# A DeltaNet and mixer kernel on one core: the written-out order of all steps is replaced by another

## The chip, the cores and the metric

The kernel runs on one core of a Trainium2 chip. A core has engines that each run their own instruction stream in order: TensorE (PE in the profile; PEld is its weight load, which overlaps the multiplication), VectorE (DVE), ScalarE (ACT), GpSimd (POOL) and SyncE (SP). Streams meet through semaphores. SP, POOL and, at the very start, ACT also issue the DMA transfers between HBM and the core's memory. The metric is the device time of one execution in microseconds. TensorE's clock is granted by a throttle, and the profile shows the granted clock (1.00 is full).

## The reference

The attention part is a delta rule with a state of 48 x 48 for each of 4 x 8 batches and heads, over 768 positions, everything in fp32; the second part mixes tokens through a rank of 32 and then runs an MLP of 384 to 1536 to 384 over channels:

```
k_n = k / (norm(k) + 1e-06)
for t in range(768):                       # q, k, v: (4, 8, 768, 48)
    y[t]  = q[t] @ state
    v_old = k_n[t] @ state
    state = state + beta[t] * outer(k_n[t], v[t] - v_old)
x  = y as (4, 768, 384)                    # heads side by side
u  = x + (x.T @ U @ V).T                   # U: 768 x 32, V: 32 x 768
out = u + relu(u @ w_ch1) @ w_ch2          # 384 x 1536, 1536 x 384
```

## The kernel before

**The work.** A sequence is cut into 12 chunks of 64 positions; six chunks of one batch's 8 heads are a *unit* n, so there are 8 units, two for each batch. For each unit the kernel

- loads k, q, v and z (a second copy of part of k), lower and upper half apart (`load`, DMA at L310; upper halves go through POOL's queue, lower ones through SP's, and the first unit's upper k through ACT's) and, once, beta (`load_beta`, L322, POOL);
- transposes k and q on PE (L218, copies at L390, L392, L395) and multiplies k by k and q by k in each chunk (`products`, L407, with copies and masks at L411 to L426);
- takes norms and beta into a scale (`norms`: square root on ACT at L353, DVE at L356 to L361) and scales v on DVE;
- inverts a unit triangular matrix for each chunk and head (`blocks`): DVE transposes the diagonal blocks (L459), substitutes column by column with one multiplication (L468) and one subtraction (L469) for each, into a tile `xt` that POOL has filled with zeros (`seed`, L454), and transposes back (L473); then PE joins the small inverses to larger ones (`joins`, L525 to L574, with ACT and DVE between). The first two units are cut into blocks of 16 (15 columns), so that the chain of DVE is short;
- runs over its chunks in order (`recur` and `outputs`, PE at L621, L628, L686, L697, L714, with DVE at L679, L704, L720, L722 and ACT at L611, L689 between). The first two units multiply k and v by the inverse ahead of time (`prepare`, L643 for k and L648 for v, ACT copies at L650, L652).

The second part's weights are loaded and converted (`start` at L790, `load_weights` with three DVE operations L809, L815, L818 and an ACT cast L796 for each of 14 slices; U is the first). For each batch and third of its tokens there are token products and a low-rank term (`front`), the first layer (`channels`, L1126 or, cut in quarters, L206), the relu on ACT (L1096), the second layer (`narrow`, L1214 or L206) and DVE's adding up (`gather`, L1160). The last batch's MLP takes another form (`quick`, L904 with DVE at L889). The second part's work of a batch stands beside the recurrence of the next, so that PE has work while the recurrence waits.

**What sets the order.** Every one of these pieces is a generator, a *part*, that stops at each instruction or short group of instructions (a *step*). A text, `ORDER`, lists one token for each step, 2342 in all. A token is the number of a part, with the PSUM bank where there is one to choose, and a `q` where a step is done in quarters. The run takes the text from left to right:

```
for token in ORDER.split():
    ...
    step = waits[int(i)]
    ...
    advance(int(i), int(bank) if bank else first)
```

So each engine's stream, and each DMA queue's, is exactly the subsequence of the text that falls to it: nothing is moved later by a scheduler. Semaphores are added from the data that instructions share; how many separate semaphore instructions an engine gets depends on the order too. A step that stands in an engine's stream and whose input isn't there holds up everything behind it on that engine.

A square root on ACT needs another function table than a copy. The last step of the first unit's upper k load is a square root of a dummy, `warm` (L315), which no other step reads:

```
if halves == (1,) and (n, name) == (0, 'k'):
    yield op('act')
    nc.scalar.sqrt(warm, warm)
```

## Time and profile before

| | |
|---|---|
| runs before | 583.02, 583.38, 586.18 us (median 583.38) |
| profiled execution, span | 581.3 us from first to last instruction; its own time is not listed apart, the median of the runs is 2.1 us more than the span |
| mean granted TensorE clock | 0.988 |
| busy: PE / PEld / DVE / ACT / POOL | 549.3 / 464.3 / 405.2 / 248.1 / 97.8 us |
| matrix instructions on PE | 11349 recorded |
| bytes moved | 33.38 MB in 63851 packets |

In the rows below, times are microseconds from the first instruction, and a line number such as L407 is a line of the kernel before. A row of the table of stretches has the stretch, its length, the busy time and the number of instructions of PE, PEld, DVE, ACT and POOL, the granted clock, the mean share of the DMA engines that are busy, and GB/s. A row of waits has the engine and line that waited, what it waited for, and us in total, number, and the longest. A row in time has the start, the duration, engine and line, operation, output and input with their shapes, and in brackets how long the engine had been idle and what ended that. A row of costly groups has the group and its count, then busy time and mean ns.

### The profile page before, as it was taken

How to read it: one execution, taken by the hardware profiler on the slowest of the kernel's cores; microseconds unless marked ns; L12 is line 12 of the kernel's file. 1: busy time of each engine (PE TensorE's matmuls, PEld its weight loads, DVE VectorE, ACT ScalarE, POOL GpSimd, SP SyncE). 2: the span in 40 equal slices, each digit the busy share in tenths (PEclk: the TensorE clock that was granted, in tenths of full speed). 3: DMA queues.
4: the chain of work that ended last, by engine and by line, in shares of the span. 5: the costliest groups of instructions: out<-in, count | busy, mean ns of one | idle time of the engine just before them, and what ended most of it. 6: DMA issues, size and time to landing. Idle time of an engine off the chain costs nothing.

```text
span 581.3 us, 25150 instructions
## 1 busy us (share of the span) xinstructions
PE 549.3 (94%) x11349; PEld 464.3 (80%) x11349; DVE 405.2 (70%) x1006; ACT 248.1 (43%) x526; POOL 97.8 (17%) x169
## 2 busy tenths in 40 slices
PE   5766999999999999999999999999999999999997
PEld 4665887669889788789879876989879869656997
DVE  6999875699998239899972899998323248157442
ACT  3678886553333553254245323631531331465000
POOL 8212150260001214221014105200000000000000
PEclk9999689999999999999999999999999999999999
DMA  9997292280000243620014204200000000000010
GB/s 146 171 249 194 75 224 54 56 151 6 30 4 16 46 76 62 111 45 3 30 24 95 61 14 85 54 29 2 31 3 2 31 2 1 28 1 0 15 41 28
DMA packets 63851, 33.38 MB, mean 57 GB/s; under 512 B 50816, under 2 KB 61824, under 8 KB 63744
## 3 DMA queue, kind: packets, MB, share of 16 engines
q1 hardware_dynamic: 56800, 23.21, 18.6%
q0 software_dynamic: 5344, 8.27, 6.6%
q8 instruction: 89, 1.46, 1.1%
q10 hardware_dynamic: 1600, 0.30, 0.3%
q14 instruction: 18, 0.15, 0.1%
HBM read 27.03 MB, written 4.72 MB: 55 GB/s over the span
## 4 chain that ended last, share of the span: by engine, by line
PE 80%; DVE 14%; issue 2%; ACT 1%; DMA 1%; SPq 0%; DVEq 0%; ACTq 0%
PE P L1214 25%; PE P L1126 13%; PE P L206 10%; PE P L904 7%; PE P L407 3%; PE P L951 3%; PE P L218 2%; DVE prod L468 2%; DVE xt L469 2%; PE P L628 2%; PE P L621 2%; PE P L686 2%; PE P L923 1%; PE P L1049 1%; PE P L673 1%
## 5 line engine op out<-in xcount | busy, mean ns | idle before, releaser
L1126 PE MATMUL P<-ut,w_sb 128*128 128x256 f32 x384 | 88.4, 385 | 0.1
L1214 PE MATMUL P<-w_sb,hs 128*128 128x192 f32 x456 | 79.9, 330 | 0.5 <-issue 0.5
L1126 PEld LDWEIGHTS P<-ut,w_sb 128*128 128x128 f32 x384 | 71.3, 190 | 11.1 <-issue 1.2
L1214 PEld LDWEIGHTS P<-w_sb,hs 128*128 128x128 f32 x456 | 74.1, 190 | 2.2 <-issue 1.3
L469 DVE TENSOR_TENSOR xt<-xt,prod 128x112 f32<-128x112 f32 (+21 forms) x200 | 64.6, 323 | 6.9
L468 DVE TENSOR_TENSOR prod<-gs,xt 128x112 f32<-128x112 f32 (+21 forms) x200 | 63.5, 318 | 2.5
L1096 ACT ACTIVATE hs<-P 128x512 f32<-128x512 f32 x48 | 28.7, 597 | 66.9 <-PE P L1126 52.4
L206 PE MATMUL P<-ut,w_sb 64*64 64x256 f32 x768 | 55.9, 383 | 0.9 <-ACT hs L1096 0.6
L1160 DVE TENSOR_TENSOR X<-X,P 128x192 f32<-128x192 f32 x85 | 29.2, 347 | 38.1 <-PE P L1214 35.2
L1214 PE MATMUL P<-w_sb,S 128*128 128x192 f32 x240 | 41.6, 329 | 0.0
L1214 PEld LDWEIGHTS P<-w_sb,S 128*128 128x128 f32 x240 | 39.0, 190 | 0.4
L407 PE MATMUL P<-slot 48*64 48x64 f32 x1536 | 34.6, 244 | 4.0 <-issue 2.0
L611 ACT COPY X<-P 64x192 f32<-64x192 f32 x96 | 30.0, 312 | 15.4 <-PE P L628 13.8
L591 POOL MEMSET slot<- 32x384 f32 x32 | 13.7, 433 | 135.7 <-PE P L562 126.0
L587 ACT COPY slot<-zz 32x384 f32<-32x384 f32 x64 | 32.2, 508 | 10.2 <-DVE zz L473 8.9
L407 PEld LDWEIGHTS P<-slot 48*64 48x64 f32 x1536 | 30.9, 156 | 7.0 <-issue 3.0
L206 PEld LDWEIGHTS P<-ut,w_sb 64*64 64x64 f32 x768 | 27.3, 133 | 9.5 <-issue 2.5
L720 DVE TENSOR_TENSOR s<-s,P 128x192 f32<-128x192 f32 x40 | 14.0, 350 | 29.8 <-PE P L714 25.0
L310 POOL DMA_DIRECT2D slot<-in_q_dram x32 | 20.9, 657 | 80.9 <-DVE prod L468 31.1
L689 ACT COPY z<-P 128x192 f32<-128x192 f32 x36 | 11.4, 318 | 53.2 <-PE P L686 45.9
L310 POOL DMA_DIRECT2D slot<-in_k_dram x44 | 29.0, 667 | 22.2 <-PE P L714 17.3
L889 DVE TENSOR_TENSOR slot<-slot,P 128x384 f32<-128x384 f32 x36 | 19.4, 553 | 19.1 <-PE P L904 18.1
(182 smaller groups left out, 1048.1 us busy)
## 6 DMA issues: line engine op xcount, KB each, us to landing
w_sb<-in_moe_w_ch_dram SPq DMA_DIRECT2D x14, 384.0 KB, 4.3
out_dram<-X SPq DMA_DIRECT2D x22, 192.0 KB, 2.0
slot<-in_k_dram SPq DMA_DIRECT2D x48, 72.0 KB, 4.1
slot<-in_k_dram POOLq DMA_DIRECT2D x44, 72.0 KB, 4.3
slot<-in_q_dram SPq DMA_DIRECT2D x32, 72.0 KB, 4.8
slot<-in_q_dram POOLq DMA_DIRECT2D x32, 72.0 KB, 4.9
slot<-in_v_dram SPq DMA_DIRECT2D x32, 72.0 KB, 3.9
slot<-in_v_dram POOLq DMA_DIRECT2D x32, 72.0 KB, 3.0
```

The costliest lines, as they stand in the source:

```text
L206: nc.tensor.matmul(to[half(g)], w[half(r), half(g)], x[half(r)], start=start, stop=stop, skip_group_check=True)
L310: queue.dma_start(out=t[half(1 - g if name == 'z' else g), :, to, 0:D], in_=src[b, 4 * g + s, hf * UC * L:(hf + 1) * UC * L, :].rearrange( ...
L407: nc.tensor.matmul(p_g[half(g ^ par * i), par, c], kq[rows, c, j, 0, half(g)], kq[rows, c, j, i, half(g)], start=True, stop=True)
L468: nc.vector.tensor_tensor(out=prod, in0=gb[:, :, j:j + 1, j + 1:].to_broadcast([128, split, m, w]), in1=xb[:, :, 0:m, j:j + 1].to_broadcas ...
L469: nc.vector.tensor_tensor(out=xb[:, :, 0:m, j + 1:], in0=xb[:, :, 0:m, j + 1:], in1=prod, op=ALU.subtract)
L587: nc.scalar.copy(pg[quarter(i), :, at, :, a:a + BK], cut(zc, h)[quarter(i)].rearrange('p r (c j) t -> p r c j t', j=2))
L611: nc.scalar.copy(x[half(c % 2), c // 2, 4 * D * g:4 * D * (g + 1)].rearrange('p (j r d) -> p r j d', r=2, d=D), states(p_y)[half(g)])
L904: nc.tensor.matmul(banks[x], w1_sb[:, 4 * a[0] + e, a[1]] if isinstance(a, tuple) else w1_mixes[a][:, e], tokens(*t) if isinstance(t, tupl ...
L1096: nc.scalar.activation(hs[:, fs[0]:fs[1] + 1:fs[1] - fs[0]], p_f, ACTF.Relu)
L1126: nc.tensor.matmul(p_f[:, x], w(x, t), ut[:, t], start=t == 0, stop=t == KT - 1)
L1160: nc.vector.tensor_tensor(out=to, in0=to, in1=p, op=ALU.add)
L1214: nc.tensor.matmul(to, of[0], of[1], start=of[2], stop=of[3], skip_group_check=True)
```

## The change

The text `ORDER` is replaced as a whole (95 lines, now 96); nothing else differs. The new text has the same multiset of steps, with the same 25 choices of quarters; only one choice of a bank differs. Because the text is one line longer, every line of code behind it has a number that is higher by one. Part numbers differ between the texts (parts are numbered as they come to life): in the part of the text shown, 1 and 0 are the first unit's k loads (the fifth token of part 1 is the square root of `warm`), 2 is beta's load with its PE and ACT steps, 147 is the load of U, 26 and 43 the upper z loads of the first two units, 36, 37 and 38, 39 the second unit's k and q, 20 the zero fill of `xt`, 146 the conversion of weights, 19 the first unit's `blocks`. The order was found with a model of the steps that also counts PE's semaphore records when it counts off lots of 256 of its instructions.

Instructions on the engines: 5913 multiplications in both texts, line by line the same; separate semaphore instructions go from 112 to 116 on PE, 136 to 129 on ACT, 177 to 173 on DVE, 62 to 56 on SP and 44 to 46 on POOL. ACT's stream has two loads of a function table instead of one: one for copies at its start, and one for square roots ahead of L353 (L354 in the new file).

```
@@ -50,95 +50,96 @@
     ORDER = """
-    1 0 1 0 1 0 1 0 2 1 36 147 37 21 150 22 36 152 153 151 149 14.3 37 21 201 2 148 201 37 36 22 36 22 21 15.1
-    20 38 202.2 148 203 39 146 148 146 204 203 2 37 21 146 205.0 202 22 154 148 202 26 38 202 29.3 39 205 149
-    39 2.1 38 205 206 205 39 2 19 202 207.3 205 2 2 2 12 17.2 202 12 207 208 19 202 12 19 205 207 19 205 209.0
-    207 19 207 19 207 3.1 19 207 3 19 209 30.2 19 18.3 209 210 19 24 23 3 3 211 19 24 38 19 24 23 3 19 24 25
...
-    714 712 718 718 714 719 715 720 715 721 721 716 722 722 723 723
+    26 147 1 1 0 0 14.0 1 1 0 201 0 15.1 202 36 43 146 37 203 201 204.2 204 202 205.3 37 204 36 36 20 29.0
+    205 206 37 2 2 146 146 38 204 205 2 2.1 2 2 149 2 37 150 43 205 22 22 22 19 22 39 39 12 2 12 19 148 148
+    205 19 19 207.0 39 207 19 19 19 207 36 30.1 208 204 38 209.3 21 21 19 19 148 148 146 19 19 209 207 17.1
+    19 209 19 21 21 39 211 18.2 19 24 209 213 210 19 146 150 209 19 146 155 19 204 204 207 19 35 205 205 3.1
...
+    11.0 11 538q 11.1 538 538 11 11.0 11 550 550 1 538 538 550 561 560 11.1 11 559.0 11.2 11 542 542 539q
...
+    711 708 708 708 713 717 713 718 714 712 719 714 710 720 715 721 718 715 594 721 716 722 722 723 723
```

(The fifth token of part 1 is the tenth token of the old text; in the new one it stands in the line shown third from the end of the diff.)

## The prediction

> **What bounds the kernel now.** I read the page's busy times first, then the stretches by time, then PE's waits in two halves, then DVE and POOL in time over the start, and last PE in time around its waits on nothing.

> ```profile
> PE 549.3 (94%) x11349; PEld 464.3 (80%) x11349; DVE 405.2 (70%) x1006; ACT 248.1 (43%) x526; POOL 97.8 (17%) x169
> ...
> PE 80%; DVE 14%; issue 2%; ACT 1%; DMA 1%; SPq 0%; DVEq 0%; ACTq 0%
> ```

> PE is busy for 549.3 of 581.3 us, and 80% of the chain that ended last is PE. The order changes no matmul, so at most the 32.0 us in which PE stood idle, and what an order costs inside PE's busy time, can be won. The stretches say where the 32 us lie (second column after the time: PE busy, fourth: DVE busy):

> ```profile
> 0.00:15.00 15.00, 7.94 (x176) 7.23 (x180) 9.29 (x36) 5.84 (x10) 12.95 (x28) 1.00 1.01 148
> 15.00:30.00 15.00, 10.89 (x256) 9.46 (x248) 13.93 (x48) 10.10 (x20) 3.22 (x5) 1.00 0.96 176
> 30.00:60.00 30.00, 21.15 (x744) 19.34 (x748) 29.21 (x77) 22.36 (x44) 6.45 (x10) 1.00 0.77 207
> 60.00:90.00 30.00, 28.07 (x842) 25.15 (x833) 23.33 (x43) 26.48 (x52) 10.31 (x16) 0.77 0.68 166
> 90.00:120.00 30.00, 28.21 (x815) 20.09 (x815) 19.53 (x42) 14.65 (x29) 8.00 (x13) 1.00 0.29 53
> 150.00:200.00 50.00, 49.49 (x1152) 43.99 (x1146) 38.21 (x99) 19.66 (x49) 4.20 (x9) 1.00 0.03 8
> ```

> Idle are 7.1, 4.1, 8.9, 1.9 and 1.8 us in the first five, some 24 of the 32, and then about 0.5 us in each 50. From 15 to 60 us DVE is busy for 43.1 of 45: it is the bound there, because the first two blocks' triangular inverses are done on it before the recurrence can start. From 60 us on PE is. PE's waits after 77 us are small:

> ```profile
> PE P L621 <- DVE s L720: 1.0, 3, 0.6
> PE P L1214 <- DVE X L1160: 0.9, 2, 0.4
> PE P L407 <- issue: 0.8, 1, 0.8
> PE P L206 <- ACT hs L1096: 0.6, 2, 0.3
> PE P L1214 <- issue: 0.5, 1, 0.5
> PE P L525 <- issue: 0.4, 1, 0.4
> ```

> Listed groups down to 0.2 us add up to some 6 us, 2 of them "issue", in which PE waited for nothing that the profile shows.

> **The change, part by part.** The program's steps are the same; each engine gets them in another order. The sum is made against the profiled execution, 581.3 us of span; the median of the runs, 583.4, lies 2.1 us above it, which I add as it is.

> *(a) The seed of the first inverse.* `norms(0)` on DVE needs both beta loads and a square root on ACT. These rows show them in before:

> ```profile
> 6.36 0.63 POOL L322 DMA_DIRECT2D X<-in_beta_dram  x1
> 3.59 1.28 ACT L315 ACT_TABLE_LOAD   x1 [3.59 <-issue]
> 15.24 0.34 ACT L337 COPY beta_rows<-P 128x48 f32<-128x48 f32 x2
> 16.03 0.18 DVE L356 TENSOR_SCALAR norm<-norm 128x32 f32<-128x32 f32 x1
> 29.00 1.96 DVE L473 STREAM_TRANSPOSE zz<-xt 128x1024 f32<-128x1024 f32 x1
> ```

> After it, POOL issues a `z` load, U, a second `z` load, two k loads, the 1.02 us fill of `xt` (L454) and a third k load ahead of both betas. At 0.66 each (U 0.86) the second beta goes out at about 8.7 instead of 6.36, and lands at about 15.0 to 15.8 (in before 6.17 us after issue, 12.53). The two copies on ACT then end near 17.8. The `warm` square root (L315), which in before loads ACT's table at 3.59 while nothing is ready, goes to near the end; the table for square roots is now loaded right ahead of L353, behind those copies: 1.28 more. The root ends near 19.4, and L356 starts near 19.45 instead of 16.03: +3.4 us. DVE has 1.2 us of other work for that time (L414, L426, which stood behind), so the inverse ends, at L473, some 2.2 us late. Against that, DVE's rows ahead of the recurrence's first copy add up to 48.03 us in the new order and 51.48 in the old: the rest, weight conversions (L809 to L818) mostly, goes behind it. From L473 to that copy before has 30.9 us of rows in 27.45 us, because rows overlap (0.89); the new order has 28.0, or 24.9 us. So the recurrence starts at 31.2 + 24.9 = 56.1 instead of 56.45: -0.4 where DVE stays dense, +2.2 where the delay stays whole. I take 0.0, near the dense end, since DVE is busy for 29.21 of 30 in that stretch.

> *(b) Waits while PE is the bound.* For each dependency I compared the time from its producer's end on PE to its reader (durations from the rows) with the PE work that stands between. Where work is short of it the order risks a wait. Behind the first 40 us of PE work these shortages sum to 52.3 us in the old order, 37.0 in the new: 30% less. They overlap and are often covered, so PE's waits after 77 us are a better base: 30% of 6 us is 1.8. Ends: 0 and -6 (all gone); I take -1.8. In the first 40 us of PE work the shortages grow from 164 to 182; DVE is the bound there, so I price this through (a).

> *(c) Changes of tile shape on PE.* A first matmul of another array shape (64*64 behind 128*128, say) starts 93 ns later than one of the same shape, at the median of the trace's rows. Shape changes go from 172 to 166: -0.6, ends -0.6 and 0.

> *(d) Lots of 256 instructions.* PE's waits on nothing all come at TensorE instruction 190 modulo 256, counted with weight loads and semaphore instructions, and the instruction queue q8 has 89 packets of 16 KB, one for each lot:

> ```profile
> 26.43 0.71 PE L407 MATMUL P<-slot 48*64 48x64 f32 x16 [1.18 <-issue]
> ...
> 118.04 0.50 PE L407 MATMUL P<-slot 48*64 48x64 f32 x17 [0.81 <-issue]
> ...
> q8 instruction: 89, 1.46, 1.1%
> ```

> Six such gaps (1.18, 0.18, 0.17, 0.81, 0.36, 0.52) cost 3.2 us. [...] In rows, no lot at full clock passes in under 3.24 us. Lots whose work is less than 3.4 us lack 3.4 us in all in the old order (12 lots) and 4.9 in the new (14); two new ones, around joins and a narrow step, hold 1.95 and 1.68 us of work. Semaphore instructions on PE go from 112 to 116 and shift every later border. I take the difference, +1.5; ends -2 (all gaps after 77 us gone) and +3.2 (both short lots at full price, 1.45 + 1.72).

> *(e) Loads of `v` for the second block.* Their upper half goes to POOL's queue behind q loads of the third block and two fills, from 50.7 and 63.5 us to about 79 and later, landing near 83. `norms(1)` scales v on DVE (1.36 us) and `prepare(0, 1)` on PE reads it, at 85.7 in before. Cover is about a microsecond: I take 0, ends 0 and +3. Behind that DVE instruction the first mixer steps are queued, which PE has other work to cover.

> *(f) Other queues.* SP's loads of the third block stand ahead of the last weight load (from 74.8 to about 78.5, still 0.7 us of PE work to spare), and a q load of the fourth behind a store of results (needed some 10 us later): 0. The tail from 550 us on keeps its steps: 0.

> Sum: 0.0 - 1.8 - 0.6 + 1.5 + 0 = -0.9, so 580.4 of span, 582.5 as a time. A measurement of this kernel can tell about 0.5%, 2.9 us, from no change: I forecast **no change that can be told**.

> **The rivals.**
> *The late seed stays (slower).* DVE was dense because each step found its input; with the chain of sixteen L468/L469 pairs 2.2 to 3.4 us late, moved conversions may have nothing left to hide behind, and PE reaches its dense part late by all of it. For it: 14% of the chain is DVE, and 3.4 us is a plain sum of rows. Against: 3.4 us less DVE work ahead of the recurrence. It decides when the first L714 matmul (54.92 in before) comes after 57. Together with the v loads of (e) at 1.5: 582.5 + 2.9 + 1.5 = 586.9.
> *Waits vanish (faster).* If the shortened shortages were the ones that cost, (b) gives -5, and if the short lots fall on waits, (d) gives 0: 583.4 - 0.4 - 5 - 0.6 = 577.4. For it: the last 400 us have 4 us of idle PE at 50 ns to 0.6 us each. Against: that is nearly all there is.
> *PE's clock.* In before PE runs at half clock from 63.30 to 76.95:

> ```profile
> 59.88:63.30 3.42, 2.38 (x120) 1.98 (x112) 3.35 (x7) 3.21 (x6) 0.70 (x1) 1.00 0.67 227
> 63.30:76.95 13.65, 12.76 (x453) 12.11 (x449) 10.67 (x26) 12.89 (x28) 1.83 (x3) 0.50 0.37 105
> ```

> 12.76 us of work at half clock are up to 6.4 at full. [...]
> *Nothing happens* is my forecast's own neighbourhood, since the terms are each under 2 us.

> **How the numbers follow.** Forecast within 0.5%: 0.40. Late seed: 0.24. Waits vanish: 0.25. Clock: 0.06 faster, 0.05 slower. So faster 0.31, same 0.40, slower 0.29. The forecast's own range is 580.5 to 586; the whole range reaches to the rivals, 577.3 to 587.5.

> **What would show it.** (a) L356 near 19.4 and L473 near 31.2, the first L714 between 54.5 and 57. (b) PE's waits after 77 us of some 4 us without "issue". (d) "issue" gaps at instruction 190 modulo 256, among them the two short lots. (e) a wait of PE on L643 or L648 between 80 and 90 us. The prediction is wrong if PE's idle time in the first 90 us moves by more than 3 us, or the half-clock window changes its length.

## The result, and the profile after

The changed kernel takes 591.7 us (median of four runs, 590.14 to 593.68) beside 584.32 for the kernel before in the same runs (583.02 to 586.18). The ratio is 1.0126, with a 95% interval of 1.0097 to 1.0156: 1.3% slower. In a second session it was 591.2, ratio 1.0117 (1.0086 to 1.0149). I had forecast 582.5 and no change that can be told; the range ended at 587.5.

The profiled execution is one of 593.68 us, the longest of the four, with a span of 592.0, 10.7 more than before; the medians lie 7.4 us apart, so this pair of profiles shows the loss some 3 us too large. The page's busy times and its chain:

```profile
PE 549.9 (93%) x11349; PEld 465.8 (79%) x11349; DVE 408.5 (69%) x1006; ACT 247.2 (42%) x527; POOL 97.7 (17%) x169
...
PE 83%; DVE 9%; issue 4%; DMA 2%; ACT 1%; POOL 1%; DVEq 0%; ACTq 0%; POOLq 0%
```

PE's busy time is the old one within 0.6 us. What grew is its idle time, from 32.0 to 42.1 us, and "issue" in the chain, from 2% to 4%. The stretches of the changed kernel (the columns as before) say where:

```profile
0.00:15.00 15.00, 6.58 (x134) 5.58 (x134) 8.36 (x32) 4.51 (x7) 11.93 (x27) 1.00 0.98 151
15.00:30.00 15.00, 8.72 (x184) 7.60 (x185) 11.45 (x42) 8.67 (x14) 3.60 (x6) 0.55 1.15 207
30.00:60.00 30.00, 20.24 (x712) 18.43 (x710) 25.81 (x66) 23.06 (x46) 7.40 (x11) 0.56 0.73 184
60.00:90.00 30.00, 24.56 (x793) 22.36 (x786) 23.86 (x55) 21.46 (x45) 3.20 (x6) 0.50 0.39 110
90.00:120.00 30.00, 29.14 (x816) 22.54 (x815) 16.20 (x31) 18.49 (x36) 10.68 (x18) 0.97 0.44 94
```

PE's idle time by stretch is 8.4, 6.3, 9.8, 5.4 and 0.9 us, beside 7.1, 4.1, 8.9, 1.9 and 1.8 before: 8.0 of the 10.1 us are lost in the first 90 us (29.9 beside 21.9), the rest behind them (12.2 beside 10.0).

The column of the granted clock (0.55 and 0.56 here, 1.00 before) is no difference between the two up to 60 us. The clock record of the kernel before begins only at 59.88, and ahead of its first entry the page shows full clock. But the same 48 records take as long there (1.56 us at 14.45 and at 33.25 us of the kernel before) as in the changed kernel, whose record says half clock, and 0.93 us when full clock is granted. First the changed kernel, then the kernel before:

```profile
31.45 1.56 PE L408 MATMUL P<-slot 48*64 48x64 f32 x48
```

```profile
115.19 0.93 PE L407 MATMUL P<-slot 48*64 48x64 f32 x48
```

So both run at half clock there; the changed kernel has two windows of 3.41 us at full clock there (from 13.01 and 53.97 us), in which PE is busy for 1.1 and 0.6 us. Full clock comes for good at 76.95 us before and at 91.51 us in the changed kernel. PE's waits in the first 77 us:

```profile
PE P L219 <- DMA slot<-in_k_dram: 6.2, 2, 5.1
PE P L574 <- issue: 4.4, 1, 4.4
PE P L563 <- DVE zz L481: 2.6, 2, 1.9
PE P L219 <- DMA slot<-in_q_dram: 2.4, 1, 2.4
PE P L334 <- DMA X<-in_beta_dram: 2.3, 2, 1.7
PE P L644 <- issue: 2.1, 1, 2.1
```

There are two waits of 4.4 and 2.1 us on nothing that the profile shows, both new, and new waits for beta and q. Another new wait, for ACT, stands at 86 us. The two waits on nothing and that one in time:

```profile
58.98 0.26 PE L574 MATMUL P<-zz 32*32 32x32 f32 x1 [4.37 <-issue]
...
65.66 1.01 PE L644 MATMUL P<-slot 64*64 64x64 f32 x27 [2.14 <-issue]
...
86.22 2.07 PE L952 MATMUL P<-ut,w_sb 128*128 128x256 f32 x4 [2.49 <-ACT X L612]
```

To see what each costs in the end I compare the kernels by work done: every step on PE counts with its median time at full clock, and the *lag* is how much later than the kernel before a kernel has done the same amount W of it. Waits, late starts and half clock all show in it, in the place where they arise. Here and below the lags are worked out from the traces of all kernels with one set of medians (before reaches W = 36 at 83 us).

| lag in us at W = | 8 | 16 | 20 | 24 | 28 | 32 | 36 | 48 | 72 | 300 | 500 |
|---|---|---|---|---|---|---|---|---|---|---|---|
| changed kernel | 4.5 | 2.2 | 6.5 | 6.1 | 5.7 | 11.4 | 11.7 | 13.0 | 9.9 | 10.9 | 10.7 |
| the same, second profile | 5.4 | 3.1 | 5.1 | 4.9 | 4.6 | 10.3 | 10.2 | 12.1 | 9.0 | 9.0 | 8.8 |

There are three jumps: about 5 us at the start, of which half is won back by W = 16; 2 to 4 us at 16 to 20, the waits on nothing; and 5.7 us from 28 to 32, where the wait on L952 lies. Behind W = 36 it grows by 2 and falls by 3, and then it is level. Each column is one execution; the two of the changed kernel differ by up to 2 us.

The traces also split a lag into idle time of PE and the rest, which is the same work done slower. This is an estimate, since it takes each step at its median. Where the kernel before stands at 46.7, 60.0, 75.0 and 82.9 us, the changed kernel lags by 1.1, 7.2, 6.5 and 11.5 us (second profile 2.0, 6.0, 5.2 and 10.1), and 1.4, 7.1, 5.5 and 8.0 us of that are idle time. So little is left of the late start at 46.7 us. The slower work comes to 3.6 us at the last place (second profile 3.1); 2.6 of them arise between 75.0 and 82.9, where the first `ahead` steps run at half clock: their multiplications follow one another every 0.43 us, and every 0.21 us in the kernel before.

### The profile page after: what moved, and what is told of

The parts are those of the page before. It is cut to its first block, busy times and chain, and to the rows that moved or that the text cites. A ratio compares the mean times of both kernels' runs of the same rounds, so it can differ in the third digit from the quotient of the medians.

```text
span 592.0 us, 25140 instructions
## 1 busy us (share of the span) xinstructions
PE 549.9 (93%) x11349; PEld 465.8 (79%) x11349; DVE 408.5 (69%) x1006; ACT 247.2 (42%) x527; POOL 97.7 (17%) x169
## 3 DMA queue, kind: packets, MB, share of 16 engines
q8 instruction: 89, 1.46, 1.1%
## 4 chain that ended last, share of the span: by engine, by line
PE 83%; DVE 9%; issue 4%; DMA 2%; ACT 1%; POOL 1%; DVEq 0%; ACTq 0%; POOLq 0%
PE P L1215 25%; PE P L1127 15%; PE P L207 11%; PE P L905 7%; PE P L408 3%; PE P L952 2%; PE P L687 2%; PE P L219 2%; PE P L629 2%; PE P L715 2%; PE P L622 2%; PE P L674 2%; PE P L1050 1%; DMA X<-in_beta_dram 1%; PE P L924 1%
## 5 line engine op out<-in xcount | busy, mean ns | idle before, releaser
L1215 PE MATMUL P<-w_sb,hs 128*128 128x192 f32 x456 | 78.4, 329 | 0.6 <-issue 0.6
L469 DVE TENSOR_TENSOR prod<-gs,xt 128x112 f32<-128x112 f32 (+21 forms) x200 | 63.7, 318 | 4.0
L207 PE MATMUL P<-ut,w_sb 64*64 64x256 f32 x768 | 51.9, 381 | 0.3 <-ACT hs L1097 0.3
L612 ACT COPY X<-P 64x192 f32<-64x192 f32 x96 | 30.0, 313 | 19.5 <-PE P L629 18.1
L408 PE MATMUL P<-slot 48*64 48x64 f32 x1536 | 33.8, 243 | 2.8 <-ACT slot L396 1.8
L396 ACT COPY slot<-P 128x768 f32<-128x768 f32 x30 | 23.4, 800 | 22.9 <-PE P L219 22.9
L690 ACT COPY z<-P 128x192 f32<-128x192 f32 x36 | 11.5, 319 | 51.2 <-PE P L687 48.4
```

What stands on the lines that cost most here:

```text
L207: nc.tensor.matmul(to[half(g)], w[half(r), half(g)], x[half(r)], start=start, stop=stop, skip_group_check=True)
L408: nc.tensor.matmul(p_g[half(g ^ par * i), par, c], kq[rows, c, j, 0, half(g)], kq[rows, c, j, i, half(g)], start=True, stop=True)
L469: nc.vector.tensor_tensor(out=prod, in0=gb[:, :, j:j + 1, j + 1:].to_broadcast([128, split, m, w]), in1=xb[:, :, 0:m, j:j + 1].to_broadcas ...
L612: nc.scalar.copy(x[half(c % 2), c // 2, 4 * D * g:4 * D * (g + 1)].rearrange('p (j r d) -> p r j d', r=2, d=D), states(p_y)[half(g)])
L1215: nc.tensor.matmul(to, of[0], of[1], start=of[2], stop=of[3], skip_group_check=True)
```

## The experiments

All edits keep the same steps and move some of them in the written order; apart from the two cuts (hyb...) and `kick`, PE's own stream is that of the kernel edited, word for word. The expectations name four theories: F, PE's code (its instructions, fetched in lots of 256: 11349 multiplications, as many weight loads and 116 semaphore instructions for the 89 packets of q8) comes late because transfers are under way; S, the late seed; B, weight conversions bunched on DVE and ACT ahead of the first `ahead` step; C, the longer half clock. The lags of all edited kernels are in one table behind the last experiment.

**1. The transfers, and code that comes late.** For each border between two lots of 256 TensorE instructions I set the time when PE crosses it beside its packet of the instruction queue q8 (one to a border, in order), with the number of transfers issued and not landed at the crossing:

| kernel | crossed at | fetch begins after | ends after | transfers under way |
|---|---|---|---|---|
| before | 48.20 | 2.21 | 3.31 | 4 |
| before | 53.96 | 2.08 | 3.11 | 3 |
| before | 58.64 | 0.94 | 2.17 | 1 |
| changed | 50.95 | 5.36 | 6.45 | 6 |
| changed | 54.41 | 8.57 | 9.62 | 8 |
| changed | 65.66 | 1.09 | 2.38 | 1 |

In the changed kernel PE runs through 256 instructions behind the first and behind the second of its crossings, and stands: for 4.37 us, until 1.58 us after the packet of 50.95 ended (57.40), and for 2.14 us, until 1.62 us after that of 54.41 (64.04). SP's queue in the changed kernel says what the transfers are (ten of weights, 384 KB each, between 48.96 and 56.7 us):

```profile
48.96 0.37 SPq L791 DMA_DIRECT2D X<-in_moe_w_ch_dram  x1
49.44 2.05 SPq L791 DMA_DIRECT2D w_sb<-in_moe_w_ch_dram  x3
51.54 0.57 SPq L791 DMA_DIRECT2D wide<-in_moe_w_ch_dram  x1
52.15 0.94 SPq L311 DMA_DIRECT2D slot<-in_v_dram  x1
53.14 1.61 SPq L791 DMA_DIRECT2D w_sb<-in_moe_w_ch_dram  x2
54.79 0.60 SPq L791 DMA_DIRECT2D X<-in_moe_w_ch_dram  x1
55.44 0.54 SPq L791 DMA_DIRECT2D w_sb<-in_moe_w_ch_dram  x1
56.02 0.63 SPq L791 DMA_DIRECT2D wide<-in_moe_w_ch_dram  x1
```

In the kernel before the same queue issues ten weight transfers from 33.8 to 47.3 us and four from 48 to 60.

`late9_10` moves four of these (SP's stream; two marks go with them, one-element writes on DVE behind which a buffer's transfer may start, in the changed kernel at 48.85 and 49.35 us with transfers from 48.96 and 49.44; they stand behind the first conversion step of slice 7):

```
 L791 DMACopy X<-in_moe_w_ch_dram 128x3x256
-L791 DMACopy w_sb<-in_moe_w_ch_dram 128x2x384
 L791 DMACopy w_sb<-in_moe_w_ch_dram 128x3x256 x2
 L791 DMACopy wide<-in_moe_w_ch_dram 128x2x384
 L311 DMACopy slot_88<-in_v_dram 64x6x48
-L791 DMACopy w_sb<-in_moe_w_ch_dram 128x2x384 x2
 L791 DMACopy X<-in_moe_w_ch_dram 128x3x256
-L791 DMACopy w_sb<-in_moe_w_ch_dram 128x2x384
+L791 DMACopy w_sb<-in_moe_w_ch_dram 128x2x384 x4
 L791 DMACopy wide<-in_moe_w_ch_dram 128x2x384
```

> The changed order with one thing moved: the six steps that load weight slices 9 and 10 (the two marks on DVE and the four transfers on SP) stand behind the first conversion step of slice 7, so that four transfers of 384 KB start some 15 us later than at 49 to 55 us. The instruction streams of PE, ACT and POOL are those of the changed kernel word for word, and so are the borders of its lots of 256. Theory F (PE's code comes late because its fetch stands behind these transfers): the two waits on nothing, 4.37 us on L574 and 2.14 us on L644, fall to under 1 us together, and the time falls by 4 to 6.5 us against the changed kernel. Theory S (the late seed costs the time): no change, within 1 us. Theory C (the longer stretch at half clock costs it): no change unless that stretch gets shorter; if the waits stay and the clock changes, C is right. If the borders themselves cost (my term d), the waits stay.

Measured: 594.58 us, ratio 1.0191 (1.0160 to 1.0222), slower still. The waits on nothing fell from 6.5 to 1.9 us (F had said under 1), and the lag at W = 24 from 6.1 to 2.0. But a new wait came in; PE's waits of this kernel in its first 100 us:

```profile
PE P L219 <- DVE zz L544: 7.9, 1, 7.9
PE P L219 <- DMA slot<-in_k_dram: 5.9, 2, 4.6
PE P L219 <- ACT slot L419: 3.6, 1, 3.6
PE P L952 <- ACT X L612: 2.9, 1, 2.9
...
PE P L574 <- issue: 1.6, 1, 1.6
```

DVE stood for 8 us ahead of L810, the conversion of the slices moved, and PE behind it. The edit showed F at its place, and its total says nothing about F's price. `late9_10b` moves the marks only behind the first conversion step of slice 6, 62.4 instead of 76 us.

> The changed order, weight slices 9 and 10 again moved to later transfers, but only as far as is needed: their marks on DVE stand behind the first conversion step of slice 6 (62.4 us in the changed kernel) instead of that of slice 7, so that they land near 70 us, ahead of their conversion at 79 us. PE's, ACT's and POOL's streams are unchanged. Theory F with the new wait of the first try (7.9 us, DVE without its weights) taken away: PE's waits on nothing between 50 and 70 us fall from 6.5 to under 2.5 us, PE's lag behind the kernel before falls from 6.6 to about 2 us at that place, and if nothing else binds the time is 4 to 5 us below the changed kernel, 587. Theory B (the conversions of slices 7 to 12, bunched between 74 and 88 us on DVE and ACT, gate the first `ahead` step whatever comes before): the gain at 70 us is lost again by 90 us and the time falls by less than 2 us.

Measured: 588.44 us, ratio 1.0114 (1.0070 to 1.0157). Waits on nothing up to 70 us are 4.2 (2.0 on L574, 2.2 on L629), the lag at W = 24 is 3.6 and at the end 4.3 instead of 10.7. The profile gains 6 us on the first profile of the changed kernel (4.5 on the second), the ratio nothing that can be told from 1.0126 and 1.0117: F has no price of its own in the times. The 4.2 us show little either. From 45 to 72 us the waits on nothing add up to 4.5 to 6.5 us in the seven profiles of the changed order with these transfers where they were, and to 1.9 to 4.9 in the six with slices 9 and 10 late.

The opposite edit, in the kernel before: `before_early` puts the transfers of slices 8, 9, 10 and half of 7 ahead.

```
 L790 DMACopy wide<-in_moe_w_ch_dram 128x2x384 x2
-L790 DMACopy w_sb<-in_moe_w_ch_dram 128x2x384
+L790 DMACopy w_sb<-in_moe_w_ch_dram 128x2x384 x4
+L790 DMACopy X<-in_moe_w_ch_dram 128x3x256
 L310 DMACopy slot_88<-in_k_dram 64x6x48
...
```

> The opposite, in the kernel before: the transfers of weight slices 8, 9 and 10 and the second of slice 7 are put ahead, so that they start as soon as their buffers are free, near 45 to 55 us, as in the changed kernel; the streams of PE, ACT and POOL stay those of the kernel before. Theory F: the code of the lots whose borders lie between 45 and 60 us comes 4 to 9 us late instead of 2 to 3, PE waits on nothing for 2 to 6 us there, and the time rises by 2 to 6 us. Theories S and C: no change, within 1.5 us, since nothing of the seed or of PE's order is touched.

Measured: 583.78 us beside 583.09, ratio 1.0002 (0.9983 to 1.0021). The border that before crosses at 48.20 is crossed at 48.25, with six transfers under way instead of four; its packet begins 7.22 us later instead of 2.21, and PE stands:

```profile
58.12 0.21 PE L573 MATMUL P<-zz 32*32 32x32 f32 x1 [3.48 <-issue]
```

So in these kernels transfers delay the code: taking them away (`late9_10`, waits on nothing from 6.5 to 1.9 us) and putting them in (`before_early`, the packet 7.22 instead of 2.21 us behind its border) both show it. But the time did not rise, where F had said 2 to 6 us: the lag is 3.2 us at W = 20 and 1.1 at the end, perhaps because weights that land sooner are in nobody's way later; no run shows that. A stall here isn't a loss of its size.

**2. The seed.** `seed_first` puts both beta loads first in POOL's queue and the dummy square root back to ACT's start; `warm_first` does the latter alone; `both` is `seed_first` with `late9_10`.

```
 L311 DMACopy slot_87<-in_k_dram 64x6x48 x4
-L391 LoadActFuncSet
+L316 LoadActFuncSet
+L316 Activation warm<-warm 128x1
...
-L354 LoadActFuncSet
 L354 Activation norm<-gs 128x32
```

> The changed order with both beta loads first in POOL's queue and the square root of the dummy, with its table load, back behind ACT's four k loads. Theory S: PE's wait for beta (2.3 us) goes, the norms on DVE start near 16 instead of 18.57, the inverse of the first unit (L474) ends 2 to 2.5 us sooner, and the time falls by 2 to 3 us. Theory F: the start gets shorter by the same amount, but the lots' code is late all the same, so the time falls by less than 1.5 us, or not at all, with PE's waits on nothing at 54 and 63 us grown or kept.

> The changed order with the square root of the dummy back behind ACT's four k loads, so that one table load at the start serves all. It takes 1.28 us off the way to the norms: they start at 17.3 instead of 18.57. If the seed's lateness goes through to the end (S), 1 to 1.3 us less than the changed kernel; if the beta loads alone matter, less than 0.5.

> Both edits, the transfers of slices 9 and 10 later and the seed first. If F and S hold and add up: 6 to 9 us less than the changed kernel, 583 to 586 and so about the time before. If only F holds: as with the transfers moved alone. If neither: the time of the changed kernel.

Measured: `seed_first` 588.06 us, ratio 1.0081 (1.0053 to 1.0109); `warm_first` 588.14, 1.0089 (1.0058 to 1.0120); `both` 591.42, 1.0145 (1.0103 to 1.0186), spoilt by the same new wait (7.7 us). The first two are 0.3 to 0.4% below the changed kernel by their ratios, some 2 us, though the intervals overlap; and not by the way that S named. DVE's rows for the norms and the end of the first inverse, changed kernel first, then `seed_first`:

```profile
18.57 0.18 DVE L357 TENSOR_SCALAR norm<-norm 128x32 f32<-128x32 f32 x1 [1.26 <-ACT norm L354]
...
31.60 2.09 DVE L474 STREAM_TRANSPOSE zz<-xt 128x1024 f32<-128x1024 f32 x1
```

```profile
17.99 0.18 DVE L357 TENSOR_SCALAR norm<-norm 128x32 f32<-128x32 f32 x1
...
31.04 2.09 DVE L474 STREAM_TRANSPOSE zz<-xt 128x1024 f32<-128x1024 f32 x1
```

The norms came 0.6 us sooner, not 2.5 (16.03 in the kernel before), and the loads that stood behind beta came later: PE's lag at W = 8 stays at 5.2. So these edits undid little of the late seed, and S was not put to the test in full. `both` has the smallest lag of these at W = 24 (1.1 us).

**3. The wait on L952.** PE's first `ahead` step writes banks that ACT has yet to empty (L612), and ACT's copies, from 85.53 us, stand behind a cast of weights (L797, 1.05 us from 84.29). `put5` moves the two copies, on ACT alone:

```
 L942 TensorCopy ut<-P 128x2x6x64
+L612 TensorCopy X<-P 64x2x2x48 x2
 L588 TensorCopy slot_88<-zz 32x2x6x32
 L797 TensorCopy w_sb<-power 128x2x384
 L566 TensorCopy zz<-P 128x192
-L612 TensorCopy X<-P 64x2x2x48 x2
```

> The changed order with one thing moved: ACT's two copies of chunk 5's outputs (L612) stand right behind the copy for `early` (L942), ahead of a cast of weights that waits for DVE. Nothing else moves on any engine. Theory B: PE's wait of 2.5 us on L952 falls to about 0.7 (the copies end near 84.4 instead of 86.2), and the time falls by 1.5 to 2 us. If the half clock (C) or DVE's backlog is what binds at this place, the time won is lost again within a few us and the total changes by less than 1 us.

Measured: 588.02 us, ratio 1.0092 (1.0068 to 1.0117), by the ratios 0.3% or some 2 us less, with overlapping intervals; the wait is 0.97 instead of 2.49. `conv_later` moves the conversions of slices 9 to 12 instead (DVE and ACT), and `all3` adds to it the seed and the transfers.

> The changed order with the conversion steps of weight slices 9 to 12 on DVE, and their casts on ACT, behind the scaling of the second unit's v instead of ahead of and among the first `ahead` steps. PE's stream is unchanged. Theory B: PE's wait on L952 for ACT (2.5 us at 86 us) goes, and the loss of some 5 us between 28 and 32 us of PE's work falls to 2 to 3; the time falls by 2 to 4 us. Theory C (half clock until 91.5 us): the loss at that place stays at 4 or more, since PE gives the same small matmuls; the time falls by less than 1.5 us. Theory F: the waits on nothing stay at 6 us in both cases.

> The changed order with the seed first, slices 9 and 10 transferred later as in the run above, and the conversions of slices 9 to 12 later. If F, S and B each hold and add up: waits on nothing under 2.5 us, no wait on L952, about 3 us won at the start, 4 to 5 at 50 to 70 us, 2 to 3 at 86 us, in all 8 to 11 us below the changed kernel, 580 to 584, level with the kernel before or a little below. If the clock (C) is the larger part: 584 to 588.

Measured: 595.36 us (1.0208, 1.0181 to 1.0236) and 591.71 (1.0152, 1.0128 to 1.0176). Both end in a wait of 5.2 us that the edit made; PE's waits of `conv_later`:

```profile
PE P L219 <- DMA slot<-in_k_dram: 6.1, 2, 4.7
PE P L644 <- ACT slot L396: 5.2, 1, 5.2
```

In `conv_later` PE has made the transposes that ACT copies (L396) by 94.9 us, but ACT copies them only at 100.68: from 93.15 to 100.14 it gives four casts of the moved conversions, three of which wait for DVE. The lag rises by 8 us between W = 36 and 48 there. Both runs say nothing on the price of B, only that this place behind isn't free for the conversions.

**4. Do the corrections add?** `f_put` is `late9_10b` and `put5`, `seed_put` is `seed_first` and `put5`, `fix3` all three; `after_again` is the changed kernel, unedited.

> The changed kernel itself, unedited, beside the next three on the same chip, so that the prices of the late seed (S), the late code (F) and the copies behind the cast (B) stand against it and not against a run of another day. Its ratio to the kernel before should lie at 1.010 to 1.016, as measured first. The corrected kernels lay at 1.007 to 1.011; if this one lies there too, none of S, F and B has a price that the time shows.

> The changed order with the transfers of slices 9 and 10 later (as in late9_10b) and the copies of chunk 5 ahead of the cast (as in put5), the seed left late. If F and B add up: 4 to 5 us below the changed kernel. If F only lets PE arrive sooner at a place where DVE, ACT or the half clock bind: as put5 alone, some 2 to 3.5 us below it.

> The changed order with the seed first and the copies ahead of the cast, the transfers left where they are. If S and B add up: 5 to 7 us below the changed kernel, within 3 us of the kernel before. If PE's late code takes the seed's gain back: 3 to 4 us below it.

> The changed order with four things set right together: both beta loads first on POOL, the dummy's square root first on ACT, the transfers of weight slices 9 and 10 behind slice 6's first conversion step, and the copies of chunk 5 ahead of the cast. If the single gains add up (3.6 for the seed, 3.3 for the transfers, 1.5 to 2 for the copies): 8 to 9 us less than the changed kernel, 582.5 to 584. If F and S are two prices for the same waiting (an earlier start only runs into the late code sooner), 585 to 588.

Measured: `after_again` 591.2 us, 1.0117 (1.0086 to 1.0149); `f_put` 589.13, 1.0075 (1.0045 to 1.0104); `seed_put` 589.06, 1.0078 (1.0050 to 1.0106); `fix3` 586.71, 1.0070 (1.0041 to 1.0098). They don't add: the pairs and all three win 0.4 to 0.6%, the single ones 0.0 to 0.4%. `fix3` still has waits on nothing of 2.9, 1.7 and 1.2 us behind 50 us and 7.2 us of lag at W = 36.

**5. Where the loss is made.** `hyb258` and `hyb487` take the first 258 or 487 steps from the kernel before (to about 52 or 90 us) and all others in the changed order.

```
 order = before[:k] + [step for step in changed if step not in before[:k]]      # k = 258, 487
```

> The first 487 steps of the kernel before (to about 90 us), then all other steps in the changed order. If the whole loss lies in the first 100 us, and the changed order is the better one behind it, as PE's lag says (it shrinks by 3.8 us from 60 us of PE's work to the end in seven of the variants, by 1.8 in the changed kernel's own profile), the time is 2 to 4 us below the kernel before: 579 to 581. If the shrinking lag only pays back work that was put off at the start, the time is that of the kernel before, within 1.5 us. If the losses at 30 to 36 us of PE's work belong to the new order's later part, it is slower than before by 2 us or more.

> The first 258 steps of the kernel before (to about 52 us, where the recurrence is about to start), then the changed order. The cut behind 487 steps took the whole loss away. If the loss is the start's alone (S, with all that follows from it), this is level with the kernel before within 1.5 us. If the stretch from 52 to 90 us has a price of its own (F, B and the half clock), it is 2 to 6 us slower than the kernel before, with PE's lag growing between 20 and 36 us of its work.

Measured: `hyb487` 583.23 us beside 582.62, 1.0011 (0.9988 to 1.0034); `hyb258` 585.83 beside 584.82, 1.0020 (0.9995 to 1.0046). So the rest of the new order is worth as much as that of the old, not more; and nearly the whole loss, 1.0 of 1.2%, goes with the first 52 us. `hyb258` keeps the wait for ACT ahead of the first `ahead` step (2.8 us) and a lag of 4.9 at W = 36, which is 2.5 by W = 72. `hyb487` gets full clock for good only at 80.69 us, 3.7 later than the kernel before; by the split of the lags its work up to there is 4.1 us slower and PE's idle time 1.9 us less, and it ends level.

**6. The clock.** `kick` adds 14 multiplications to the changed kernel, to raise PE's activity while it runs at half clock:

```
+    nc.vector.memset(P[:, 1, 384:512], 0.0)
+    def kick():
+        for _ in range(KICKS):
+            yield op('pe')
+            nc.tensor.matmul(P[:, 1, 384:512], ident, ident, start=False, stop=True, skip_group_check=True)
```

> The changed order with 14 added multiplications of 128*128 by 128 columns (two records of 128 columns each) spread over PE's steps between the end of the second inverse and the first `ahead` step; they write columns that nothing reads. They cost 14 x 0.38 us = 5 us at full clock if they stood in a dense stream, about twice that at half clock. In six traces so far a window of 3.41 us at half clock was followed by full clock exactly where columns times array share (full 128*128 columns) reached 1149 or more, and stayed at half up to 1144; windows there hold 780 to 990. With two or three added ones (256 each) they hold 1300 or more. Theory C: the clock is granted some 15 us sooner (near 71 to 75 us instead of 91.5), and the time rises by less than 2 us or falls. If a window is judged by PE's busy time alone: no earlier grant, and the time rises by 4 to 8 us.

Measured: 610.77 us, 1.0491 (1.0441 to 1.0541). An added record took 500 ns at the median, so the 28 cost 14 us, and the first grant of full clock in the trace is at 97.6 us, behind the first `ahead` steps (94.09). The lasting grant comes behind them in all other edited orders too, but in the kernel before it stands 0.4 us ahead of them (76.95 and 77.34). Between the first added record and that grant one window of 3.41 us with 1280 columns, over my 1149, was not followed by full clock: my rule of a threshold falls. The run's other 5 us aren't explained, and it doesn't measure the price of the half clock; the split of the lags above, 3 to 4 us by 82.9 us, is all there is.

The lags of the edited kernels (us), from the same medians as above, one execution each:

| | W = 8 | 16 | 24 | 36 | 72 | 500 |
|---|---|---|---|---|---|---|
| late9_10 / late9_10b | 5.4 / 5.1 | 3.0 / 2.5 | 2.0 / 3.6 | 14.6 / 8.2 | 13.8 / 5.6 | 11.4 / 4.3 |
| seed_first / warm_first | 5.2 / 5.3 | 1.6 / 1.7 | 3.5 / 2.4 | 8.4 / 7.2 | 7.1 / 4.7 | 5.0 / 2.5 |
| put5 / fix3 | 5.2 / 5.2 | 2.9 / 2.1 | 5.0 / 3.5 | 8.8 / 7.2 | 6.3 / 6.0 | 5.0 / 5.0 |
| f_put / seed_put | 5.5 / 4.8 | 3.2 / 1.6 | 3.3 / 4.8 | 6.4 / 7.9 | 6.2 / 6.5 | 4.9 / 5.8 |
| before_early / hyb258 / hyb487 | 0.3 / 0.5 / 0.2 | 0.1 / 0.0 / 0.0 | 2.5 / -0.3 / 1.0 | 3.1 / 4.9 / 2.3 | 2.5 / 2.5 / 2.6 | 1.1 / 2.3 / 1.8 |

## Why the prediction was wrong

The failed step is the price of the start: (a) put it at 0.0, and (f) put the transfers at nothing. The runs show a loss there instead: `hyb258`, which gives back the order of the first 52 us, takes away 1.0 of the 1.2%, and between 46.7 and 60.0 us of the kernel before PE's idle time grows by 5.7 us more than in that kernel (second profile 4.4). What the sum had no term for is the transfers' effect on PE's code: (f) "Other queues" looked only at loads that could come too late for their readers, and (d) at lots that are too short. Neither asked what else the transfers delay. In (a) I let weight conversions go behind the recurrence as a gain of DVE time. But a weight transfer waits for a one-element mark on DVE, and from slice 7 on for the conversion that frees its buffer. Marks and conversions stand later in DVE's new order, so ten transfers went out together at 49 to 57 us; there PE passes two borders within 3.5 us, and its code came 5.4 and 8.6 us late. That transfers delay the code was shown by `late9_10` and `before_early`. That this chain makes the loss is argued only, from the cut at 258 steps, which brings back the early transfers among much else: no run gave a price for the late code alone, and in `before_early` it had none. Both of the prediction's own signs of being wrong came true: PE's idle time in the first 90 us rose by 8.0 us, and the half clock lasted longer, to 91.51 us instead of 76.95.

Point by point:

- (a) The way to the norms and the inverse was right: L357 at 18.57 (predicted 19.4), L474 at 31.60 (31.2). By its own mark the step held up to there. The first L715 then came at 59.54 instead of 54.5 to 57, and 4.37 us of that is the wait on L574 just ahead of it: without it, some 55.2 (second profile 57.66 with a wait of 1.8, so some 55.9). What the lateness cost in the end isn't told by the runs apart from the rest: 0.5 us at the norms went with some 2 us of time and with smaller waits on nothing (4.5 in `warm_first`, instead of 6.5 and, in the second profile, 5.0).
- (b) Wrong: predicted -1.8. PE's listed waits behind 90 us add up to 7.7 us beside 5.8 before, its idle time there to 12.2 beside 10.0, and `hyb487` wins nothing. Smaller shortages of cover didn't become less waiting: those that cost were few, and I had no means to tell them.
- (c) 0.6 us: too small for any run to show.
- (d) Behind 90 us, where I had priced it, it was right: gaps at instruction 190 or 191 of a lot cost 3.3 us beside 2.0, +1.3 of +1.5 predicted. It was applied only where transfers are few. Of the waits on nothing that it puts all at instruction 190, one stands elsewhere (0.62 us at 22.24 us of the kernel before). These traces have crossings that cost from nothing to 4.4 us, the dearest with six to eight transfers under way.
- (e) Right: no wait for v at 80 to 90 us. A wait stands there all the same (L952, 2.5 us), of a kind that I had not looked for: two ACT copies behind a cast. `put5` priced it at some 2 us (ratio 1.0092 against 1.0117 and 1.0126, not beyond the intervals).
- The rival "late seed stays" named the right place and sign and 586.9, and its mark, a first L714 after 57, came true; but at 46.7 us only 1 to 2 us of lag were left, and the rest came behind, with the waits on nothing. Of the rival "PE's clock" the sign came true, a half clock of another length: full clock comes for good at 91.51 us instead of 76.95. No run shows what sets the half clock off, so the rival's two chances, 0.06 and 0.05, rest on no run; the traces show when full clock comes for good (76.95 us in the kernel before, 80.69 in `hyb487`, 91.51 in the changed kernel) and, by the split, some 3 to 4 us of slower work by 82.9. (The prediction's 63.30 to 76.95 is the end of a longer half clock, which the rows of 1.56 us show at 14.45 and 33.25 us already, with one window of full clock from 59.88; it had read the missing record as full clock.) In `f_put`, `seed_put` and `fix3` the wait on L952 is about 1 us or less and the lag still rises, by 2.6 to 3.3 us between 75.0 and 82.9 us of the kernel before; by the split 0.7 to 1.0 of it is idle time and 2.0 to 2.7 slower work, which I put down to the half clock. What that costs in the end no run tells.

What stays open is the split. Undoing 52 us of the order takes away 1.0 of 1.2%; the three corrections that leave PE's order alone take away 0.4 to 0.6% in any combination. The remainder may lie in how the new start lets transfers, borders and DVE's work meet; no single moved step settles it.

## What to carry to other kernels

## What the runs showed of the hardware that I had not expected

The start of a fetch behind its border, by transfers under way at the crossing, between 44.9 and 80 us in five traces (before, changed, `fix3`, `hyb258`, `before_early`): 0.6 to 2.0 us with none or one, 1.0 to 3.1 with two or three, 0.4 to 4.6 with four or five, 3.2 to 8.6 with six or more, but for two crossings with seven and eight at 0.6 and 1.2 us. The number of transfers is thus a coarse measure. In the three stalls shown PE goes on 1.4 to 1.6 us after the packet has ended.

In the changed kernel 10.24 us of a busy PE brought no full clock. The kernel at half clock, up to the lasting grant:

```profile
57.38:67.62 10.24, 5.96 (x200) 5.39 (x202) 5.97 (x17) 3.96 (x7) 0.00 (x0) 0.50 0.68 201
67.62:77.86 10.24, 10.24 (x361) 10.04 (x359) 6.68 (x17) 8.99 (x21) 0.00 (x0) 0.50 0.02 4
77.86:91.51 13.65, 10.89 (x288) 9.00 (x285) 11.20 (x22) 10.35 (x21) 4.67 (x9) 0.50 0.68 169
91.51:95.00 3.49, 3.49 (x62) 2.85 (x61) 2.75 (x5) 1.39 (x3) 3.45 (x6) 1.00 0.57 111
```

For 10.24 us PE was busy without a break and stayed at half clock; the 361 instructions were of tiles of 48*64 to 64*64. The grant came 5.3 us behind the first multiplication of 128*128 (86.22). In the kernel before it came at 76.95, 0.4 us ahead of the first one (77.34), so there it came without one. The record's stretches at half clock last 13.65 us in the kernel before (63.30 to 76.95) and 37.55 and 34.13 in the changed one (16.42 to 53.97, 57.38 to 91.51), 4, 11 and 10 times the 3.41 us of the shortest stretch at full clock. Three such 3.41 us in a row, from 67.62 to 77.86, were busy by the profile's rows and brought no grant.
